# Half of the first keys loaded through GpSimd's casting queue instead of SyncE's queue, with new instruction orders

## The chip, the cores and the metric

The kernel runs on one core of a Trainium2 chip. A core has five engines with instruction rows of their own: PE (TensorE, matrix multiplies; PEld is its weight load), DVE (VectorE), ACT (ScalarE), POOL (GpSimd) and SP (SyncE). DMAs are issued from SP, ACT or POOL and share 16 DMA engines. Those that POOL issues here also change the type of the data on the way (float32 to bfloat16). The metric is device time of one execution in microseconds (us); lower is better.

## What is computed

Pooled attention over 8 batches and 8 heads (576 positions, head size 64; keys and values are averaged over 8 neighbouring positions, so 72 of each), and then a gated feed-forward net: a hidden layer of 1024 with ReLU, a convolution over three positions, a sigmoid gate, and an output layer of 512.

```
def _attn_ref(q, k, v):
    k_p = k.reshape(B, H, Sp, pool, D).mean(axis=3)
    v_p = v.reshape(B, H, Sp, pool, D).mean(axis=3)
    scores = scale * np.matmul(q, k_p.transpose(0, 1, 3, 2))
    scores = scores - np.max(scores, axis=-1, keepdims=True)
    attn = np.exp(scores)
    attn = attn / (np.sum(attn, axis=-1, keepdims=True) + 1e-09)
    return np.matmul(attn, v_p)

def _moe_ref(x, w_in, conv_w, w_out):
    h = np.maximum(x @ w_in, 0.0)
    hp = np.concatenate([zeros, h, zeros], axis=1)
    for k in range(K):
        conv_out += conv_w[k][None, None, :] * hp[:, k:k + S, :]
    gate = 1.0 / (1.0 + np.exp(-conv_out))
    return h * gate @ w_out
```

## The kernel before

The kernel is written as a graph of some 1040 small operations. Each is a Python closure that issues a handful of instructions, with a list of the operations it needs. `Graph.order` walks the table `ORDER`: an entry is twice an operation's number plus 0 or 1, the bit choosing between two engines where an operation may run on either; -1 puts in a spare, a dummy matmul (`fill`, L424) that computes nothing of the result. `FORMS` picks for some PE operations between a form with few wide matmuls and one with many narrow ones, and `PLACES` gives the buffer or PSUM bank. The tables fix the row of every engine; each engine takes its row strictly in order, and an instruction waits until what it needs is done.

The batches go in four groups of two. For each batch: the values are pooled in three additions and spread over masked columns (`prep_v`, L511 and L515, DVE). The keys are pooled; for the first two batches by matmuls against a pool matrix (`prep_k`, L431 and L441) with a copy out of PSUM (`copy_k`, L456), for the other batches by additions (L464) and turning matmuls with copies (L483, L504). The queries are transposed on PE (`prep_q`, L541 in the wide form, L545 in the narrow) and copied (`copy_q`, L559), or for two batches transposed by DMA (L553). Then for each tile of up to 128 positions: scores (`att_scores`, L620 wide, L607 narrow), maximum (L633, DVE), subtraction (L653 on PE or L645 on DVE), exponential (L682, ACT), transposition (L692 with the copy L706, or the DMA L701), product with the values (L717), reciprocal (L730), division (L745 on DVE, or eight parts at L738 on ACT), and transposition of the result (L762 with the copy L770, or the DMA L754). The feed-forward part of a batch: the hidden layer (`ffn_in`, L775, PE), ReLU (L784, ACT), and the convolution. This runs on PE (L939) with tanh (L964) for most of the first batches, or, for blocks of four 128-row pieces listed in `TAPS` (batches 4 to 7), as two multiply-adds on DVE, the taps (`ffn_tap`, L911), with the gate function on ACT (L921). Taps read columns beyond the tile's ends, which two small copies (`ffn_wrap`, L859 and L860, on POOL or ACT) fill. The gate is multiplied in (`ffn_times`, L989, DVE), and the output layer (L997, PE) is copied out of PSUM (L1008) and stored (L1020).

All loads but three are casting DMAs of POOL, in POOL's row: L284 for keys and queries of one batch, L291 for keys of a pair, L317 and L320 for values, L327 and L335 for weights. The exceptions concern batch 0. Its keys come in two pieces of two partition-major quarters each (`heads` 0 to 2 and 2 to 4), and its queries in two pieces along the row (`cs` 0 to 4 and 4 to 9). Both key pieces and the first query piece are loaded as float32 by SP (`load_raw`, L299) into room of `hT`, and cast to bfloat16 by DVE or ACT (`cast_raw`, L306) in steps of two quarters. The second query piece goes by POOL's casting queue. In `add_load` one condition (L1073) makes this choice. `prep_k` of batch 0 runs in two halves of 18 matmuls, the first needing the first key piece, the second the other; L1199 names the operation of each piece.

PE's row before begins with 15 fills, then 8 matmuls of the first query piece, the 36 of both key halves, the remaining 8 of the first query piece with the 20 of the second, and then the scores of the first tile.

Of the kernel before, what the change touches and what calls it, by code (L numbers as in the profile page):

```python
# [33 lines left out]
class Graph:  # L34
# [148 lines left out]
def kernel(  # L183
# [883 lines left out]
    def add_load(kind, b, key, share=1.0, after=(), **part):  # L1067
# [5 lines left out]
        if b == 0 and (kind == "k" or part["cs"].start == 0):  # L1073
            heads, cs = part.get("heads", slice(0, 4)), part.get("cs", slice(0, C))
# [424 lines left out]
```

## Time and profile before

| what | us |
|---|---|
| median of three runs | 213.53 |
| lowest, highest | 212.31, 215.35 |
| the profiled execution, its own time | 213.68 |
| span of that execution, first to last instruction | 211.7 |
| busy in it: PE / DVE / ACT / POOL | 198.9 / 190.5 / 167.2 / 36.7 |

The time of an execution holds the span and what lies around it. Busy times come from the one profiled execution. A matmul's duration is that of its way through the array, and the next one starts before it ends, so a busy PE may still have room. In a group's row stand the source line, the engine, the operation, the tiles, the count, the busy us, the mean duration in ns of one, and after the bar the idle time of the engine ahead of these instructions, with what ended it.

### The profile page before, as it was taken

How to read it: one execution, taken by the hardware profiler on the slowest of the kernel's cores; microseconds unless marked ns; L12 is line 12 of the kernel's file. 1: busy time of each engine (PE TensorE's matmuls, PEld its weight loads, DVE VectorE, ACT ScalarE, POOL GpSimd, SP SyncE). 2: the span in 40 equal slices, each digit the busy share in tenths (PEclk: the TensorE clock that was granted, in tenths of full speed). 3: DMA queues.
4: the chain of work that ended last, by engine and by line, in shares of the span. 5: the costliest groups of instructions: out<-in, count | busy, mean ns of one | idle time of the engine just before them, and what ended most of it. 6: DMA issues, size and time to landing. Idle time of an engine off the chain costs nothing.

```text
span 211.7 us, 6644 instructions
## 1 busy us (share of the span) xinstructions
PE 198.9 (94%) x2726; PEld 136.4 (64%) x2746; DVE 190.5 (90%) x338; ACT 167.2 (79%) x345; POOL 36.7 (17%) x60
## 2 busy tenths in 40 slices
PE   4899999999999999999999899999999999999990
PEld 1468788765688876776778675666666656654450
DVE  7879988999999999999998989999999999999520
ACT  2558677998999869999979977989899997889030
POOL 8604630052131110200000021000014400202000
PEclk9999999999999999999999999999999999999997
DMA  6999999999999999879663646756646626204985
GB/s 212 222 205 206 208 206 208 208 207 205 208 206 208 202 179 202 177 139 156 130 92 69 147 96 78 173 104 151 122 96 133 113 64 149 53 0 103 261 259 171
DMA packets 48834, 33.47 MB, mean 158 GB/s; under 512 B 28300, under 2 KB 43812, under 8 KB 48804
## 3 DMA queue, kind: packets, MB, share of 16 engines
q0 software_dynamic: 15216, 15.40, 44.6%
q1 hardware_dynamic: 32432, 15.93, 35.9%
q10 hardware_dynamic: 1156, 1.72, 2.8%
q8 instruction: 21, 0.34, 0.6%
q14 instruction: 9, 0.07, 0.1%
HBM read 32.52 MB, written 9.44 MB: 198 GB/s over the span
## 4 chain that ended last, share of the span: by engine, by line
PE 68%; DVE 19%; issue 5%; ACT 4%; DMA 2%; DVEq 0%; ACTq 0%
PE psum L997 25%; PE psum L775 22%; PE psum L717 5%; PE psum L939 3%; DVE negm L633 3%; DVE v L511 2%; PE psum L692 2%; DMA eT<-e 2%; PE psum L424 2%; DVE sd L645 2%; DVE gT L981 2%; PE psum L620 2%; DVE gT L989 1%; PE psum L653 1%; PE psum L762 1%
## 5 line engine op out<-in xcount | busy, mean ns | idle before, releaser
L775 PE MATMUL psum<-xT,w_in_sb 128*128 128x288 bf16 x512 | 72.0, 286 | 0.2
L997 PE MATMUL psum<-w_out_sb,gT 128*128 128x512 bf16 (+1 forms) x276 | 65.6, 373 | 1.4 <-issue 0.6
L775 PEld LDWEIGHTS <-w_in_sb 128*128 128x128 bf16 x512 | 47.8, 98 | 15.3
L784 ACT ACTIVATE hT<-psum 128x576 bf16<-128x576 f32 x64 | 41.1, 669 | 8.0 <-PE psum L775 7.8
L997 PEld LDWEIGHTS <-gT 128*128 128x128 bf16 x296 | 27.5, 98 | 26.5 <-DVE gT L989 0.5
L633 DVE TENSOR_REDUCE negm<-psum 128x8 f32<-128x576 f32 (+2 forms) x37 | 27.4, 750 | 2.0 <-ACT e L682 0.9
L921 ACT ACTIVATE gT<-tg,ratio 128x576 bf16<-128x576 f32 x28 | 21.6, 795 | 2.2 <-DVE tg L911 2.1
L911 DVE SCALAR_TENSOR_TENSOR tg<-hT,ratio,tg 128x576 f32<-128x576 bf16 x28 | 22.3, 813 | 0.7
L911 DVE SCALAR_TENSOR_TENSOR tg<-hT,ratio 128x576 f32<-128x576 bf16 x28 | 22.2, 812 | 0.2 <-ACT gT L921 0.2
L859 POOL COPY hT<-hT 128x126 bf16<-128x126 bf16 x7 | 5.7, 808 | 93.8 <-ACT hT L784 74.9
L989 DVE TENSOR_TENSOR gT<-gT,hT 128x2304 bf16<-128x2304 bf16 x16 | 21.6, 1354 | 0.2
L645 DVE TENSOR_TENSOR sd<-psum,negm 128x576 f32<-128x576 f32 x27 | 19.9, 751 | 0.6
L717 PE MATMUL psum<-vm,eT 128*128 128x65 bf16 (+5 forms) x240 | 19.0, 222 | 0.9 <-DMA eT<-e 0.9
L738 ACT ACTIVATE x<-psum,r 128x64 bf16<-128x64 f32 (+1 forms) x80 | 17.6, 352 | 2.8 <-DVE r L730 2.7
L682 ACT ACTIVATE e<-sd 128x576 bf16<-128x576 f32 x27 | 18.6, 703 | 0.4 <-DVE sd L645 0.2
L745 DVE TENSOR_TENSOR x<-psum,r 128x512 bf16<-128x512 f32 (+1 forms) x27 | 18.2, 682 | 0.5
L717 PEld LDWEIGHTS <-eT 128*128 128x128 bf16 (+1 forms) x240 | 15.1, 100 | 5.3 <-DMA eT<-e 1.7
L939 PE MATMUL psum<-hT,dw 64*64 64x288 bf16 (+2 forms) x576 | 17.0, 256 | 0.3 <-ACT qT L559 0.2
L939 PEld LDWEIGHTS <-dw 64*64 64x64 bf16 x576 | 13.9, 107 | 3.4 <-issue 2.3
L424 PE MATMUL psum<-gT 128*128 128x448 bf16 x40 | 13.1, 433 | 3.2 <-DVE gT L1106 2.8
L1008 ACT COPY osb<-psum 128x512 f32<-128x512 f32 x24 | 14.3, 600 | 1.2 <-PE psum L997 1.2
L511 DVE TENSOR_TENSOR v<-v 128x1280 bf16<-128x1280 bf16 (+2 forms) x24 | 12.9, 538 | 0.2
(95 smaller groups left out, 244.8 us busy)
## 6 DMA issues: line engine op xcount, KB each, us to landing
out_dram<-osb SPq DMA_DIRECT2D x54, 128.0 KB, 2.5
v<-in_v_dram POOLq DMA_DIRECT2D x8, 512.0 KB, 12.6
qp<-in_q_dram POOLq DMA_DIRECT2D x7, 576.0 KB, 15.3
kk<-in_k_dram POOLq DMA_DIRECT2D x3, 1152.0 KB, 13.7
out_dram<-qp ACTq DMA_DIRECT2D x12, 128.0 KB, 3.4
hT<-in_k_dram SPq DMA_DIRECT2D x2, 576.0 KB, 5.2
w_in_sb<-in_moe_w_in_dram POOLq DMA_DIRECT2D x2, 512.0 KB, 13.7
w_out_sb<-in_moe_w_out_dram POOLq DMA_DIRECT2D x1, 1024.0 KB, 23.7
```

The lines of the kernel that those rows point to most:

```text
L633: nc.vector.tensor_reduce(out=a["m"][0:rows], in_=a["s"][0:rows, :, 0:2 * KW].rearrange("p a (h s) -> p a h s", s=Sp), axis=AX.X, op=OP.ma ...
L645: nc.vector.tensor_tensor(out=a["d"][0:rows], in0=a["s"][0:rows, :, 0:2 * KW].rearrange("p a (h s) -> p a h s", s=Sp), in1=a["m"][0:rows]. ...
L682: nc.scalar.activation(out=dst, in_=src, func=ACT.Exp,)
L717: nc.tensor.matmul(out=a["o"][lo:hi, h // 4, (h % 4) * (D + 1):(h % 4 + x1 - x0) * (D + 1)], lhsT=a["eT"][:, j, lo:hi], rhs=buf("vm", b)[: ...
L745: nc.vector.tensor_tensor(out=a["x"][0:rows].rearrange("p (a h d) -> p a h d", a=2, d=D), in0=ov[:, :, :, 0:D], in1=r[0:rows].unsqueeze(3) ...
L775: nc.tensor.matmul(out=banks(ps)[:, j, 0:SC], lhsT=w_in_block(dc, fb), rhs=buf("xT", g)[:, dc, i * S + j * SC:i * S + (j + 1) * SC], start ...
L784: nc.scalar.activation(out=h_of(b)[:, fb].rearrange("p (a s) -> p a s", a=2), in_=banks(ps)[:, :, 0:SC], func=ACT.Relu, scale=1.0 if (b, f ...
L911: nc.vector.scalar_tensor_tensor(out=acc, in0=h, scalar=w, in1=acc if tap else mid, op0=OP.mult, op1=OP.add)
L921: nc.scalar.activation(out=gate, in_=acc_of(b, fb, ps), func=squash(b, fb), scale=ratio[:, 1, fb:fb + 1])
L939: nc.tensor.matmul(out=banks(pss[r ^ c])[c * D:(c + 1) * D, j, lo:hi], lhsT=dw[r * D:(r + 1) * D, tap * n_fb + fb, :], rhs=hT[r * D:(r + 1 ...
L989: nc.vector.tensor_tensor(out=gate, in0=gate, in1=h_of(b)[:, four], op=OP.mult)
L997: nc.tensor.matmul(out=bank(ps)[0:rows, columns], lhsT=buf("gT", g)[:, fb, t * P:t * P + rows], rhs=w_out_sb[:, fb, columns], start=(fb == 0),
```

## The change

`add_load` now lets only the first key piece of batch 0 (`heads` from 0) go by SP and a cast; the second (`heads` 2 to 4) falls through to the general case, a casting DMA of POOL (`load_k`, L284) straight into the bfloat16 tile. So the graph has one operation less: the SP load with its cast operation is replaced by one load. The tables `ORDER`, `FORMS` and `PLACES` are new from the first entry to the last; all the planner's other settings are as they were.

```
-        if b == 0 and (kind == "k" or part["cs"].start == 0):
+        if b == 0 and (part["heads"].start == 0 if kind == "k" else part["cs"].start == 0):
             heads, cs = part.get("heads", slice(0, 4)), part.get("cs", slice(0, C))
             d = add({"SP": 0.5}, key, lambda: load_raw(raw, heads, cs), land=(0.6, kb * share, RATE_FIRST))
             cast = []
...
     ORDER = (
-        0, 12, 10, 24, 16, 4, 44, 28, 8, 36, 14, 32, 46, 19, -1, -1, -1, -1, 21, 7,
+        0, 14, 4, 22, 42, 10, 12, 8, -1, -1, -1, -1, -1, -1, -1, 6, 40, 30, 34, 36,
...
     FORMS = (
-        0, 0, 0, 0, 1, 1, 1, 1, 0, 0, 0, 0, 0, 1, 1, 0, 1, 1, 0, 0, 1, 0, 1, 0, 0, 0, 0, 1, 0, 0, 0, 1, 1, 1, 1, 1, 1, 1, 0, 1,
+        1, 0, 0, 0, 1, 1, 1, 0, 0, 0, 0, 1, 1, 1, 1, 0, 0, 0, 1, 1, 0, 0, 0, 1, 1, 0, 0, 1, 0, 0, 0, 1, 1, 1, 1, 1, 1, 1, 0, 1,
...
```

Counted over the whole rows: fourteen wrap pairs (L859 and L860) stand 7 on ACT and 7 on POOL before, 2 and 12 after. DVE has 4 of the wide query copies (L559) before and 2 after, 7 and 5 of the wide output copies (L770), 26 and 25 of the wide divisions (L745); ACT has 6 and 8, 10 and 12, and 72 and 80 parts of divisions (L738). Of the casts of batch 0, DVE has one of the keys before and one of the queries after; ACT has one of the keys and two of the queries before, and one of each after. The number of fills is 40 in both.

PE's row after begins with 8 fills, the 18 matmuls of the first key half, 4 fills, the 16 of the first query piece, the 18 of the second key half, the 20 of the second query piece, and then the scores of the first tile in the narrow form.

The places of which the prediction speaks, with the names of the program's tiles: POOL's row behind the constants at the program's start (`ident` the identity, `mask` the head mask, `gT` whose spare room holds the pool matrix, `qp` the queries, `kk` the keys). Before:

```order
masks.py:197 MEMSET ident 128x128
masks.py:199 ISA
masks.py:199 AFFINE_SELECT ident<-ident 128x128
L362 MEMSET mask 128x15
L364 AFFINE_SELECT mask<-mask 128x15 x2
L343 AFFINE_SELECT gT_122<-gT_122 64x9x72 x2
L284 DMA qp_76<-in_q_dram 128x4x320
```

and after:

```order
L284 DMA kk_78<-in_k_dram 128x2x576
masks.py:197 MEMSET ident 128x128
masks.py:199 ISA
masks.py:199 AFFINE_SELECT ident<-ident 128x128
L362 MEMSET mask 128x15
L364 AFFINE_SELECT mask<-mask 128x15 x2
L343 AFFINE_SELECT gT_122<-gT_122 64x9x72 x2
L284 DMA qp_76<-in_q_dram 128x4x320
```

The key load stands ahead of everything else; the other seven rows keep their order. DVE's row at the end of its set-up, where the first results of PE come in (`ident_k` the scaled identity, `pick` its rearranged columns, `kT` the pooled keys, `qT` the transposed queries). Before:

```order
L359 COPY gT_122<-gT_122 64x9x72
L384 TENSOR_SCALAR ident_k<-ident 128x128
L387 COPY pick<-ident_k 128x2x16 x4
L306 CAST kk_78<-hT_116 128x1152
L456 CAST kT_82<-psum 64x2x72
L559 COPY qT_79<-psum 128x2x256
L559 COPY qT_79<-psum 128x2x320
L633 TENSOR_REDUCE negm_95<-psum 128x8
```

and after:

```order
L306 CAST qp_76<-hT_117 128x2x256
L339 MEMSET kT_82 128x288
L376 TENSOR_SCALAR vm_90<-mask 128x15
L376 TENSOR_SCALAR vm_91<-mask 128x15
L376 TENSOR_SCALAR vm_92<-mask 128x15
L376 TENSOR_SCALAR vm_93<-mask 128x15
L376 TENSOR_SCALAR vm_94<-mask 128x15
L456 CAST kT_86<-psum 64x2x72 x3
L559 COPY qT_80<-psum 128x2x320
L633 TENSOR_REDUCE negm_97<-psum 128x8
```

The key cast is gone from DVE and a query cast is there; `ident_k` and `pick` stand some 40 rows later, behind the first attention tiles. ACT's row from its first cast on. Before:

```order
L306 CAST qp_76<-hT_117 128x2x256 x2
L306 CAST kk_78<-hT_116 128x1152
L559 COPY qT_79<-psum 128x2x256
L456 CAST kT_82<-psum 64x2x72 x3
L559 COPY qT_79<-psum 128x2x320
```

and after:

```order
L306 CAST kk_78<-hT_116 128x1152
L456 CAST kT_86<-psum 64x2x72
L306 CAST qp_76<-hT_117 128x2x256
L559 COPY qT_80<-psum 128x2x256 x2
L559 COPY qT_80<-psum 128x2x320
```

The one key cast left on ACT is that of the first piece, ahead of the query cast.

More of the change, by code (lines that the diff above doesn't have):

```diff
@@ L72 @@
     ORDER = (
[54 rows of a table removed]
[54 rows of a table added]
     )
     FORMS = (
-        0, 0, 0, 0, 1, 1, 1, 1, 0, 0, 0, 0, 0, 1, 1, 0, 1, 1, 0, 0, 1, 0, 1, 0, 0, 0, 0, 1, 0, 0, 0, 1, 1, 1, 1, 1, 1, 1, 0, 1,
+        1, 0, 0, 0, 1, 1, 1, 0, 0, 0, 0, 1, 1, 1, 1, 0, 0, 0, 1, 1, 0, 0, 0, 1, 1, 0, 0, 1, 0, 0, 0, 1, 1, 1, 1, 1, 1, 1, 0, 1,
     )
     PLACES = (
[18 rows of a table removed]
[18 rows of a table added]
     )
@@ L1072, in add_load @@
             toks[b] = token("qp", b)
-        if b == 0 and (kind == "k" or part["cs"].start == 0):
+        if b == 0 and (part["heads"].start == 0 if kind == "k" else part["cs"].start == 0):
             heads, cs = part.get("heads", slice(0, 4)), part.get("cs", slice(0, C))
```

144 rows, old and new, of tables (ORDER, PLACES) are left out of this document.

## The prediction

> **What bounds the kernel now.** First the busy time by stage (columns: stretch in us, its length, busy us and instruction count of PE, PEld, DVE, ACT and POOL, granted clock, DMA share, GB/s), cut where the chain changes its nature: end of the loads' casts, first score matmul, first hidden-layer matmul, first tap, last gate, last matmul.
>
> ```profile
> 9.44:11.71 2.27, 2.10 (x65) 2.03 (x66) 0.85 (x3) 1.67 (x6) 0.00 (x0) 1.00 1.19 185
> 11.71:28.09 16.38, 16.35 (x346) 12.22 (x346) 14.90 (x31) 11.29 (x19) 6.67 (x9) 1.00 1.23 207
> 28.09:125.00 96.91, 94.40 (x1631) 71.12 (x1633) 92.61 (x168) 85.02 (x175) 11.50 (x20) 1.00 1.01 172
> 125.00:197.04 72.04, 71.31 (x626) 44.06 (x632) 70.87 (x101) 63.49 (x141) 10.62 (x14) 1.00 0.53 105
> 197.04:205.90 8.86, 8.78 (x48) 4.62 (x48) 2.96 (x5) 2.24 (x4) 0.00 (x0) 1.00 0.89 271
> 205.90:211.70 5.80, 0.00 (x0) 0.00 (x0) 0.42 (x1) 0.00 (x0) 0.00 (x0) 0.81 0.58 174
> ```
>
> From 11.71 us on PE is busy nearly throughout, and DVE almost as much: 70.87 of 72.04 us in the late stretch, where PE has 71.31. Two engines are full together, so relief of one alone is worth little, and a wait on either shows. The clock is 1.00 until the matmuls end; it plays no part.
>
> Second, the chain that ended last, at its start and inside the middle stretch (start us, us, what).
>
> ```profile
> 7.47 0.59 DVE ident_k L384
> 8.09 0.70 DVE pick L387 x4
> 8.79 0.61 DVE kk L306
> 9.44 1.33 PE psum L431 x36
> 10.80 0.27 ACT kT L456
> ...
> 11.71 0.41 PE psum L620 x4
> 12.12 0.65 PE psum L424 x3
> ...
> 90.18 0.81 DVE v L511
> 91.00 0.77 DVE negm L633
> ```
>
> Up to 9.4 us the chain is DVE's list of small set-up work, ending in the cast of the first keys; then PE pools the keys (L431), ACT copies them (L456), and the first scores (L620) start at 11.71. Around 90 us the chain runs on DVE; late it is PE.
>
> Third, the first loads and casts themselves, from the timeline, and the landing times (the last number of an issue group, and the min/median/max of SyncE's three loads).
>
> ```profile
> 1.83 0.52 SPq L299 DMA_DIRECT2D hT<-in_k_dram  x1
> 3.59 0.89 POOL L284 DMA_DIRECT2D qp<-in_q_dram  x1
> 5.27 1.15 DVE L381 COPY mask_wide<-mask 128x960 bf16<-128x960 bf16 x1
> 5.74 0.81 POOL L284 DMA_DIRECT2D kk<-in_k_dram  x1
> 6.05 1.14 ACT L306 CAST qp<-hT 128x512 bf16<-128x512 f32 x2 [3.66 <-DMA hT<-in_q_dram]
> 8.40 0.98 DVE L306 CAST kk<-hT 128x1152 bf16<-128x1152 f32 x1
> 8.62 1.15 ACT L306 CAST kk<-hT 128x1152 bf16<-128x1152 f32 x1 [1.43 <-DMA hT<-in_k_dram]
> 10.59 0.95 PE L541 MATMUL psum<-ident,qp 128*64 128x128 bf16 x28
> ...
> qp<-in_q_dram POOLq DMA_DIRECT2D x1, 320.0 KB, 6.6
> kk<-in_k_dram POOLq DMA_DIRECT2D x1, 576.0 KB, 10.6
> DMA to landing us min/median/max: 3.7/4.7/6.8
> ```
>
> SyncE's second key half, issued at 1.83, landed 6.8 us later, at 8.6, where ACT stops waiting for it and casts until 9.77. The casting load of the other five ninths of the first queries, issued at 3.59, landed 6.6 us later, at 10.2. The first key half (3.7 us) was there by about 4.5, and was cast only at 8.40: DVE was not free.
>
> **The change part by part.** (1) *The load moves.* GpSimd issues it first of all, at the 0.8 us where its first memset of the identity stood, and pushes everything behind it back by one issue, about 0.8 us (0.89 and 0.81 above): identity, mask, pool matrix, and the casting loads of queries, first values and second keys on the same queue. SyncE's queue then holds one key half and the queries, in the same order. The landing is the unknown. From below: bytes shared with SyncE's two loads, 3.7 to 4.7 us as those took, so 4.5 to 5.5. From above: 10.6 us as the second keys' casting load took with three loads ahead of it, so 11.4. I take 6.6 us, the query load of the same queue, which likewise shared the engines with SyncE's loads: 7.4, inside the 8.6 of before.
>
> The first queries' second part comes behind it on the queue. Before, that part landed at 10.2 after the same four pieces of data (two key halves, two query parts); after, the same four. I take 10.2 again; bounds 9.4 (the 0.8 us of later issue gained back as the values no longer push in) and 11.1 (10.2 and one issue).
>
> A rule speaks against the move. The Trainium skill, "SBUF — State Buffer", section "SBUF: two separate sides", holds that a GpSimd-issued DMA waits for its descriptors while VectorE runs a copy in a two-port mode, and the next section gives 620 ns alone against 3100 ns beside such a copy. Here the issue at 5.74 stood beside the 1.15 us copy at L381 and took 0.81, against 0.89 for one beside memsets: the trace doesn't show the rule. By the rule's figures the landing would be an estimated 2.5 us later, 9.9 in place of 7.4.
>
> (2) *The casts go.* ACT's 1.15 us cast of the second half (8.62 to 9.77) is gone, and DVE's 0.98 us cast of the first moves to ACT, which has been idle for 3.66 us by 6.05. DVE takes one of the two query casts (1.14 for two), and its identity scaling and `pick` (0.59 and 0.70, on the chain) go to a place behind the first attention tiles. DVE's set-up list is no longer in front of the keys. In PE's row stand now: first key half, 4 fills, first query part, second key half, second query part, first scores. The fills and key half are done by about 7 (cast from 4.5 to 5.65, 18 of the 36 pool matmuls, 0.66 us); the second key half by 8.1 (7.4 and 0.66); so the second query part, landing at 10.2, is late next. Its 20 of 28 matmuls take 0.68, and the scores start at 10.9 in place of 11.71: **0.8 us gained**. With the bounds, 9.4 gives 1.6 gained; 11.1 gives 0.1 lost. If the keys land at 11.4, 0.66 of pooling, three copies on DVE in place of ACT's three at 0.27, and 0.68 put scores at 13.5: 1.8 lost.
>
> (3) *The new orders shift work between engines.* Counted in the rows of both orders, priced by the groups of before (name, shapes, count, busy us, mean ns; two lines give min/median/max ns instead):
>
> ```profile
> L559 DVE COPY qT<-psum 128x1152 bf16<-128x1152 bf16 x4 | 3.0, 740 | 0.0
> L770 DVE COPY xT<-psum 128x512 bf16<-128x512 bf16 x7 | 2.9, 420 | 0.4 <-PE psum L762 0.2
> L745 DVE TENSOR_TENSOR x<-psum,r 128x512 bf16<-128x512 f32 x26 | 17.6, 682 | 0.5
> L738 ACT ACTIVATE x<-psum,r 128x64 bf16<-128x64 f32 x72 | 15.9, 357 | 2.4 <-DVE r L730 2.3
> L559 ACT COPY qT<-psum 128x1152 bf16<-128x1152 bf16 x6 | 6.7, 1120 | 0.3 <-PE psum L541 0.2
> L770 ACT COPY xT<-psum 128x512 bf16<-128x512 bf16 x10 | 5.8, 583 | 2.4 <-PE psum L762 2.4
> L483 ACT CAST kT<-psum 64x288 bf16<-64x288 f32 x8 | 3.0, 392 | 0.1
> L859 ACT COPY hT<-hT 128x126 bf16<-128x126 bf16 x7 | 2.2, 310 | 0.1
> L859 POOL COPY hT<-hT x7: 292/827/1472, 125.8 to 190.0; 128x126 bf16<-128x126 bf16 x7
> L911 DVE SCALAR_TENSOR_TENSOR tg<-hT,ratio x28: 765/810/900, 124.2 to 192.2; 128x576 f32<-128x576 bf16 x28
> ```
>
> DVE gives up the key cast (0.98), two query copies (2 x 0.74), two output copies (2 x 0.42), one division (0.68) and a narrow query copy (0.3, 512/1152 of 0.74): 4.3. It takes one query cast (0.5, between 512/1152 of its 0.98 and half of ACT's 1.14) and five key copies (two small at ACT's 0.27, three at 0.39): 2.2. Net **-2.1 us on DVE**. ACT gives up a query cast, those five copies and ten wrap copies (0.57 + 1.7 + 10 x 0.31 = 5.4) and takes two query copies, two output copies, a division in eight parts and the narrow copy (2 x 1.12 + 2 x 0.58 + 8 x 0.36 + 0.5 = 6.8): +1.4. GpSimd takes the ten wrap copies at about 0.82: +8.2, on an engine with 10.62 busy of the late 72.04 us.
>
> What is DVE's relief worth? Late, where PE is as full, nothing. In the middle, where the chain runs on DVE, up to all of it. Bounds 0 and 2.1; I take half, **1.0 gained**, since PE has 94.40 of 96.91 there. ACT's 1.4 has cover: 85.02 of 96.91 and 63.49 of 72.04 us busy.
>
> (4) *Fills.* PE's row holds dummy matmuls (L424) where a gap was planned: 40 in both, but 28 instead of 25 after the first scores, and 12 instead of 8 after the first hidden layer matmul. At 0.22 each (0.65 for three) three more cost 0.7 if PE had work, nothing if it waits; I take **0.6 lost**, as PE waits little. PE's other work: half of one query preparation in 18 wide instead of 36 narrow matmuls, and scores of three tiles the other way; at 0.41 a tile that can't be over 1.2 either way, taken as nothing.
>
> (5) *What counting can't give.* Each of the new orders' thousand steps waits for others; the measure is PE's idle time of before after 28 us, 2.51 + 0.73 = 3.2 us. A new order could close all of it, or have twice as much; I take a little more, **0.6 lost**, bounds -3.2 and +3.2.
>
> The end is alike: after the last two gates (L989) PE's row has the same 32 wide and 16 half output matmuls, so the 8.86 and 5.80 us of the last two stretches stay.
>
> Sum: -0.8 - 1.0 + 0.6 + 0.6 = -0.6. The profiled execution took 213.68 us, of which
>
> ```profile
> span 211.7 us, 6644 instructions
> ```
>
> leaves 2.0 around it, unchanged; it stands 0.15 above the median, 213.53. So 213.68 - 0.6 = 213.1.
>
> **The rivals.** *Slower, by the wraps.* Ten wrap copies go to GpSimd, where a pair takes 1.65 (2 x 0.827) instead of 0.62 on ACT. DVE's taps (L911) of that block can't begin before. If in all five pairs the first tap stands next in DVE's row, DVE waits 1.03 each, 5.2 in all, in the stretch where it has 1.2 idle: 213.1 + 5.2 = 218.3, over 2% slower. It decides only if all five wait; four give 217.2. For it: GpSimd's copies stretch to 1.47. Against: none of before's seven pairs there shows a DVE wait, and taps of several blocks interleave. That GpSimd and VectorE hinder each other here is also what the Trainium skill, "SBUF — State Buffer", section "Who interferes with whom", holds for a VectorE instruction with two SBUF inputs beside a GpSimd read, and L859's 292 to 1472 agrees; L911, 765 to 900, bounds the loss on DVE's side at 0.1 for each tap it meets. Chance 0.06. *Slower by other waits of the new orders*: as much idle again as before had, 3.2, with the start's 1.8 lost and no relief for DVE: 213.68 + 3.2 + 1.8 + 0.6 = 219.3. Chance 0.12.
>
> *The late load.* The keys land at 11.4, the start loses 1.8 in place of gaining 0.8: 213.1 + 2.6 = 215.7, within 2%. For it: the second keys took that on this queue; against: they had three loads ahead of them, these have none. Chance 0.12. By the rule of (1) it would be 9.9 and, with the pooling, copies and the second query part behind it, scores at about 12: 214.2.
>
> *Nothing at the start.* The second query part holds the scores and the gain is used up by a fill or a copy: 213.9. Chance 0.15.
>
> *Faster.* All of DVE's 2.1 counts, the start gains 1.6 and the idle falls by half, 1.6, fills costing nothing: 213.68 - 5.3 = 208.4. Chance 0.12.
>
> **How the numbers follow.** The forecast, 0.43, with the late load and the unchanged start makes 0.70 for within 2%, which is about what a measurement of this kernel can tell from no change (212.31 to 215.35 over three runs, 1.4%), here 209.3 to 217.8. Slower 0.06 + 0.12 = 0.18, faster 0.12. The range leaves out about a tenth at each side: from 209.4, most of the faster case beyond it, to 217.9, just short of the two slow ones.
>
> **What would show it.** Right: the first L620 or L607 near 10.9 us, behind the second query part and not behind the keys; GpSimd's first load landing by 8; DVE's busy time about 2 us below before's, GpSimd's about 8 above; PE's idle from 28 us to the last gate near 4. Wrong: L431 waiting for the key load at 9 us or later; a DVE wait at L911 for L859 or L860; PE idle over 6 us between 28 and 197.

## The result and the profile after

| what | before | after |
|---|---|---|
| median, us (4 runs each) | 213.49 | 215.67 |
| lowest, highest | 212.31, 215.35 | 215.22, 217.20 |
| profiled execution, its span | 213.68, 211.7 | 215.22, 213.5 |
| busy PE / DVE / ACT / POOL | 198.9 / 190.5 / 167.2 / 36.7 | 200.6 / 189.0 / 168.4 / 40.3 |

The change is slower by 1.4%: ratio 1.0136, 95% interval 1.0104 to 1.0168. A second measurement, beside later experiments, gave 1.0118 (1.0060 to 1.0177). In the tables below medians are over all runs, while ratios leave disturbed ones out, so the two can differ.

The busy time of after in the stretches in which before was shown (same columns):

```profile
9.44:11.71 2.27, 1.16 (x46) 0.90 (x40) 0.69 (x3) 1.20 (x3) 0.86 (x2) 1.00 1.17 167
11.71:28.09 16.38, 15.56 (x352) 11.36 (x344) 14.69 (x31) 12.02 (x25) 6.18 (x8) 1.00 1.23 207
28.09:125.00 96.91, 95.18 (x1656) 71.81 (x1646) 92.16 (x173) 84.42 (x165) 12.30 (x22) 1.00 1.02 169
125.00:197.04 72.04, 71.75 (x631) 44.08 (x630) 69.84 (x99) 63.33 (x142) 12.94 (x22) 1.00 0.58 113
197.04:205.90 8.86, 8.65 (x42) 3.83 (x41) 4.24 (x6) 3.04 (x6) 0.00 (x0) 1.00 0.71 203
205.90:211.70 5.80, 1.69 (x16) 1.27 (x13) 0.85 (x2) 0.59 (x1) 0.00 (x0) 0.82 0.80 230
```

PE has work at 206 us where before it had none. It is idle for longer up to 28 us (1.16 busy of 2.27, 15.56 of 16.38), and for less afterwards. Two places of the timeline show where it stands still. The first is the start:

```profile
1.32 0.84 POOL L284 DMA_DIRECT2D kk<-in_k_dram  x1 [0.80 <-POOLq L1483]
4.97 0.77 POOL L284 DMA_DIRECT2D qp<-in_q_dram  x1
...
10.84 0.75 PE L541 MATMUL psum<-ident,qp 128*64 128x128 bf16 x20 [1.11 <-DMA qp<-in_q_dram]
11.52 0.33 PE L607 MATMUL psum<-kT,qT 64*64 64x72 bf16 x16
```

The issue groups of the same start (the last number is us to landing):

```profile
qp<-in_q_dram POOLq DMA_DIRECT2D x1, 320.0 KB, 5.8
kk<-in_k_dram POOLq DMA_DIRECT2D x1, 288.0 KB, 6.1
```

The keys land at 1.3 + 6.1 = 7.4. The second query part is issued at 4.97, where before it was at 3.59; it lands at 10.8, and PE waits for it. The second place is near 90 us (bracket: idle before, and what ended it):

```profile
84.68 1.32 SPq L701 DMA_TRANSPOSE eT<-e  x1
86.05 2.50 SPq L1020 DMA_DIRECT2D out_dram<-osb  x4
88.65 3.82 SPq L553 DMA_TRANSPOSE qT<-qp  x1
...
90.42 0.44 PE L692 MATMUL psum<-ident,e 128*128 128x128 bf16 x5
91.78 1.04 PE L997 MATMUL psum<-w_out_sb,gT 128*128 128x512 bf16 x4 [0.92 <-issue]
```

"issue" means that PE waited for nothing that the profile knows of. `eT` are the transposed exponentials, `osb` the output buffers.

To see how far a kernel has come, the matmul columns that PE has still to start are counted from the trace's weight loads and divided by a round 2400 a us (in after's trace one 512-column matmul of L997 mostly starts 0.216 us behind the other, which is 2370). The difference to before, in us of PE work that a kernel is behind, is good to some 0.4, since the orders differ:

```
from, us              30    60    80    90    95   100   110   150   200
after                1.0   0.4   0.4   1.1   1.8   1.3   2.0   1.0   1.7
after, again         1.6   1.0   1.3   1.8   1.9   1.6   2.3   1.3   2.1
load alone          -0.2  -0.1   0.0  -0.1   1.0   1.8   2.3   1.3   1.3
load, L553 late     -0.2  -0.1   0.0  -0.1  -0.2   0.3   0.8  -0.4  -0.2
orders alone         0.6  -0.1   0.0   0.7   1.4   1.2   1.6   0.6   1.3
orders, short keys   0.4  -0.1   0.0   0.2   0.2  -0.2   0.1  -0.9  -0.2
```

The start and the stretch from 85 to 100 us carry the loss.

### The profile page after: what moved, and what is told of

It is laid out like the page before. It is cut to its first block, busy times and chain, and to the rows that moved or that the text cites. A ratio compares the mean times of both kernels' runs of the same rounds, so it can differ in the third digit from the quotient of the medians.

```text
span 213.5 us, 6693 instructions
## 1 busy us (share of the span) xinstructions
PE 200.6 (94%) x2756; PEld 136.6 (64%) x2756; DVE 189.0 (89%) x337; ACT 168.4 (79%) x342; POOL 40.3 (19%) x71
## 5 line engine op out<-in xcount | busy, mean ns | idle before, releaser
L775 PE MATMUL psum<-xT,w_in_sb 128*128 128x288 bf16 x512 | 70.2, 286 | 0.4 <-DVE x L745 0.2
L997 PE MATMUL psum<-w_out_sb,gT 128*128 128x512 bf16 (+1 forms) x296 | 67.0, 373 | 1.1 <-issue 0.9
L775 PEld LDWEIGHTS <-w_in_sb 128*128 128x128 bf16 x512 | 48.3, 98 | 15.3 <-issue 1.2
L997 PEld LDWEIGHTS <-gT 128*128 128x128 bf16 x296 | 27.8, 98 | 29.2 <-issue 1.1
L859 POOL COPY hT<-hT 128x126 bf16<-128x126 bf16 x12 | 6.4, 534 | 98.1 <-ACT hT L784 92.6
L738 ACT ACTIVATE x<-psum,r 128x64 bf16<-128x64 f32 (+1 forms) x88 | 19.2, 328 | 1.8 <-DVE r L730 1.6
L745 DVE TENSOR_TENSOR x<-psum,r 128x512 bf16<-128x512 f32 (+1 forms) x26 | 17.9, 687 | 0.6
L1008 ACT COPY osb<-psum 128x512 f32<-128x512 f32 x24 | 14.1, 599 | 1.1 <-PE psum L997 1.0
L964 ACT ACTIVATE tg<-psum 128x576 bf16<-128x576 f32 x18 | 11.7, 652 | 2.8 <-PE psum L939 2.8
## 6 DMA issues: line engine op xcount, KB each, us to landing
v<-in_v_dram POOLq DMA_DIRECT2D x8, 512.0 KB, 11.1
qp<-in_q_dram POOLq DMA_DIRECT2D x7, 576.0 KB, 14.1
```

What stands on the lines that cost most here:

```text
L738: nc.scalar.activation(out=a["x"][0:rows, n * D:(n + 1) * D], in_=ov[:, n // 4, n % 4, 0:D], func=ACT.Identity, scale=r[0:rows, n // 4, n ...
L775: nc.tensor.matmul(out=banks(ps)[:, j, 0:SC], lhsT=w_in_block(dc, fb), rhs=buf("xT", g)[:, dc, i * S + j * SC:i * S + (j + 1) * SC], start ...
L997: nc.tensor.matmul(out=bank(ps)[0:rows, columns], lhsT=buf("gT", g)[:, fb, t * P:t * P + rows], rhs=w_out_sb[:, fb, columns], start=(fb == 0),
```

## The experiments

All compare with the kernel before on the same chip.

| kernel | median, us | ratio | 95% interval |
|---|---|---|---|
| load alone | 215.91 | 1.0098 | 1.0065 to 1.0131 |
| orders alone | 214.48 | 1.0060 | 1.0041 to 1.0080 |
| new start, old rest | 218.68 | 1.0227 | 1.0164 to 1.0290 |
| old start, new rest | 213.94 | 1.0044 | 1.0029 to 1.0059 |
| before, 288 KB more on GpSimd's queue | 216.04 | 1.0133 | 1.0091 to 1.0174 |
| load alone, L553 late | 213.67 | 1.0019 | 0.9991 to 1.0047 |
| before, L553 late | 213.56 | 1.0013 | 1.0000 to 1.0027 |
| after, 64 rows more | 219.72 | 1.0304 | 1.0251 to 1.0357 |
| after, stores early | 216.19 | 1.0156 | 1.0115 to 1.0196 |
| orders alone, stores early | 214.49 | 1.0057 | 1.0035 to 1.0079 |
| after, 12 fills out | 216.80 | 1.0117 | 1.0077 to 1.0158 |
| orders alone, 12 fills out | 214.38 | 1.0059 | 1.0030 to 1.0088 |
| orders alone, 288 KB more | 215.34 | 1.0109 | 1.0072 to 1.0146 |
| orders alone, short keys | 213.06 | 0.9991 | 0.9969 to 1.0013 |
| after, short keys | 215.86 | 1.0144 | 1.0123 to 1.0165 |

**Load or orders.** *Load alone*, in the rows of SyncE, GpSimd and ACT, everything else as before (k0 and q0 are the first parts of batch 0's keys and queries, k0+ and q0+ the second):

```
-  SP: k0, q0, k0+      POOL: ident, mask, pool matrix, q0+, ...
+  SP: k0, q0           POOL: k0+, ident, mask, pool matrix, q0+, ...
-  ACT: cast of k0+
```

> The old orders, slots and forms; only the load of the second half of the first keys goes from SyncE's queue to GpSimd's, first on that queue, and its cast on ScalarE is gone. Theory A (the new orders cost the time, the load by itself is nearly free): the keys land near 7.4 us as in the changed kernel, the second query part about 0.8 later than before because GpSimd's row is 0.84 longer ahead of it, first scores between 11.2 and 12.2 us, total within 0.6 of the kernel before (213.0 to 214.1). Theory B (the moved load costs the time, by delaying the second query part or by slowing VectorE's set-up): first scores at 12.7 or later and a total of 214.9 to 215.7, like the changed kernel.

*Orders alone* is after with this undone:

```
+  SP: k0, q0, k0+      POOL: ident, mask, pool matrix, q0+, ...
+  ACT: cast of k0+ behind the cast of the first query part
```

> The new orders, slots and forms; only the load goes back to SyncE's queue, third on it, with its cast on ScalarE behind the cast of the first query part. Theory A (the new orders cost the time): 215.0 to 216.2, as the changed kernel, with the gap of PE near 91 us in the trace. Theory B (the load costs it): 213.0 to 214.0.

Neither theory had it: both parts cost, and nearly add up (1.0098 x 1.0060 = 1.0158). In the load alone the first scores start at 11.58, no later than before's 11.71, and it is not behind until 90 us; its whole loss comes between 90 and 110.

**Start or rest.** The two orders were joined at the first hidden-layer matmul (L775), with buffers found anew where the halves meet:

```
-  ORDER = after's
+  ORDER = after's up to the first L775, then before's (and the reverse, with the old load)
```

> The new load and the new orders up to the first hidden layer matmul of batch 0 (L775), the old orders from there (36 fills in all, 32 of them at the start where the new order has them). Theory A1 (the loss lies behind the first 30 us: transitions and the stall near 91 us): 213.2 to 214.2. Theory A2 (the start loses, 1.0 us of PE work behind at 30 us, and it is never made up): 214.4 to 215.2.

> The old load and the old orders up to the first hidden layer matmul, the new orders from there (44 fills in all). Theory A1 (the loss lies behind the first 30 us): 214.9 to 216.2, with the gap of PE near 91 us. Theory A2 (the start loses): 213.2 to 214.3.

Both theories missed the first (218.68; PE waits 2.57 us for ACT's L1008 at 97.68 in it, a wait that the load alone shows below), and the second came out where A2 had it. That doesn't show A2's reason, since ahead of the gap near 91 us its PE program is 24 rows shorter, and the gap is gone. The pair also moves the load along with the start, so it does not tell the parts apart.

**Why a load at 1.3 us costs at 90.** The two pages' rows of GB/s (40 slices of the span, 5.3 us each), before and load alone:

```profile
GB/s 212 222 205 206 208 206 208 208 207 205 208 206 208 202 179 202 177 139 156 130 92 69 147 96 78 173 104 151 122 96 133 113 64 149 53 0 103 261 259 171
```

```profile
GB/s 212 155 198 207 207 206 208 207 207 206 208 207 207 204 110 141 165 251 122 159 103 61 153 109 82 141 109 162 113 103 147 102 74 148 52 0 97 255 260 178
```

From the third slice to the fourteenth it stays near 207: GpSimd's queue is full to some 74 us. Before, the second slice held 222, as SyncE's loads came on top; with the load moved it holds 155, and each of GpSimd's later loads lands later, by 1.0 to 1.5 us from 38 to 73 us. The query load of batch 6 (576 KB), issued at 58.69 in before, landed after 14.1 us, at 72.8; issued at 58.48 in the load alone it took 15.4, to 73.8. What waits for it is SyncE's DMA transposition of batch 6 (L553), which starts 0.1 us behind the landing in both. SyncE's row before:

```profile
72.83 3.64 SPq L553 DMA_TRANSPOSE qT<-qp  x1
81.29 1.20 SPq L701 DMA_TRANSPOSE eT<-e  x1
82.54 2.51 SPq L1020 DMA_DIRECT2D out_dram<-osb  x4
```

and in the load alone, with two rows of its PE and ACT below:

```profile
73.92 10.72 SPq L553 DMA_TRANSPOSE qT<-qp  x1
84.75 2.67 SPq L701 DMA_TRANSPOSE eT<-e  x1
87.47 2.98 SPq L1020 DMA_DIRECT2D out_dram<-osb  x4
...
95.50 0.58 ACT L1008 COPY osb<-psum 128x512 f32<-128x512 f32 x1 [1.72 <-DMA out_dram<-osb]
96.14 1.02 PE L997 MATMUL psum<-w_out_sb,gT 128*128 128x512 bf16 x3 [1.46 <-ACT osb L1008]
```

GpSimd issues the next key pair (1152 KB) at 73.51 in before, 0.7 behind L553; in the load alone at 73.31, 0.6 ahead of it. Issued behind that load, the transposition holds SyncE for 10.72 us in place of 3.64. The stores behind it come 5 us late, ACT waits for an output buffer, and PE for ACT.

Three runs test this. One more load on the queue, behind all that the start waits for:

```
     def load_w_in(j):
+        if j == 0:
+            load_more()     # 288 KB of keys, cast into a part of hT that nothing reads
```

> The kernel before, with its keys still loaded by SyncE, and one more load of the same 288 KB on GpSimd's queue (the same rows, cast into a part of hT that nothing reads) just ahead of the first half of w_in, so behind all that the start waits for. Theory Q (GpSimd's queue is full without a break from 5 to 73 us, so that 288 KB more on it make every later load land about 1.0 to 1.4 us later; the query load of batch 6 then lands behind the issue of the next key pair, the DMA transposes of L553 run beside that load for some 10 us in place of 3.6, and SyncE's transposes and stores behind them come late): L553's issue takes over 8 us, first scores as before at 11.7, total 214.0 to 216.5, and runs that lie further apart than before's. Theory S (the moved load costs at the start): 212.5 to 213.6, L553's issue below 5 us.

L553, issued 1.5 us behind the key pair's load, held SyncE for 8.56 us; first scores came at 11.68 as before, and the time was 216.04: the loss without the moved load. Then the transposition out of the way, with its control:

```
-  SP: L553, L701 (eT), 4 x L1020, ...
+  SP: L701 (eT), 4 x L1020, L553, ...
```

> The load moved in the old orders, as in the run of the load alone (1.0098 of before), and in addition the first DMA transposes of L553 (batch 6) behind the next eT transposes and the four output stores on SyncE's queue. Theory Q (they block SyncE for 10.7 us beside the key pair's load): the eT transposes are issued near 81.3 again and not at 84.7, PE loses under 1.0 between 85 and 100 us, total 212.6 to 214.0. Rival (the lost time is the load's elsewhere, at the start or in PE's own row): as with the load alone, 214.5 to 216.

> The kernel before with only that move of L553 behind the eT transposes and the four stores: the control for it. Both theories: 212.3 to 214.0, since before's L553 runs in 3.6 us where nothing else is on the queues; if the later place costs something by itself (it then meets the loads of v at 86 us), up to 214.5.

With L553 late the load costs 1.0019 against the control's 1.0013. PE's busy time from 90 to 100 us, in the load alone and with L553 late:

```profile
90.00:95.00 5.00, 3.79 (x109) 2.98 (x109) 4.55 (x8) 2.88 (x5) 0.00 (x0) 1.00 0.99 224
95.00:100.00 5.00, 3.81 (x33) 2.33 (x37) 3.74 (x8) 4.36 (x13) 0.00 (x0) 1.00 0.67 155
```

```profile
90.00:95.00 5.00, 5.00 (x122) 3.63 (x121) 4.84 (x10) 4.66 (x9) 0.00 (x0) 1.00 1.25 172
95.00:100.00 5.00, 4.54 (x62) 2.62 (x58) 4.90 (x12) 4.71 (x14) 0.00 (x0) 1.00 1.13 174
```

Theory Q holds for the old orders: 7.60 busy of 10 becomes 9.54. In the new orders L553 stands at 88.65, where it took 3.82, so this cost can't be theirs.

**The gap near 90 us.** The trace lists 21 packets of 16 KB of instructions, and PE's program has some 5500 rows, one packet to about 251 of them (eight packets between rows 3260 and 5268 in after). The gap stands at the same row in kernels in which different instructions stand there. Numbers from the traces; the row 252 ahead marks the packet's turn. The gap is counted from the start of the weight load ahead of it to the start of the next, so it is longer than the idle time in the profile's bracket:

```
kernel                  PE at row   packet  behind   GpSimd's loads    PE's gap ahead of
                          2752      starts             landed          row 3004 to 3006
before                    85.72     86.88    1.16    85.5               none
load, L553 late           85.50     87.12    1.62    83.8               none
load alone                85.52     88.87    3.35    87.9               0.64 (16 L607, ahead of the 6th)
after                     86.12     89.14    3.02    88.8 and 89.2      1.19 (L997)
after, again              86.74     89.67    2.92    89.3 and 89.8      0.99 (L997)
orders alone              85.69     88.69    3.00    88.4 and 88.8      1.18 (L997)
after, stores early       86.85     89.97    3.12    89.6 and 90.1      1.21 (L997)
orders, stores early      85.09     88.19    3.09    87.8 and 88.3      1.18 (L997)
orders, 288 KB more       86.48     89.28    2.81    88.9 and 89.4      0.93 (L997)
orders, short keys        85.24     86.26    1.02    84.7 and 85.0      none
after, short keys         87.06     87.98    0.92    87.1 and 87.4      none
old start, new rest       85.84     88.84    3.00    88.5 and 89.0      none (PE there at 91.6)
after, fills out          86.25     89.26    3.02    88.9 and 89.4      none (PE there at 92.0)
orders, fills out         86.80     89.45    2.65    89.1 and 89.6      none (PE there at 92.3)
```

Where there is a gap, PE goes on 1.4 to 1.5 us after the packet has landed. In the last three kernels the packet is late too. But their program is 24 rows shorter up to there, so four wide matmuls (L997) stand in front of row 3004, and PE comes to it only 1.5 to 1.7 us after the packet has landed. The Trainium skill, "Runtime: NRT & Kernel Launch", section "Instruction fetch mechanics", has blocks of 16 KiB, which an engine's sequencer fetches through its own DMA queue while it runs the one before, "mostly hidden". The trace agrees on size and way (21 packets of 16 KB on a queue of their own); here it was not hidden, by up to 1.2 us.

A first test moved the fetch, by 32 tiny matmuls (64 rows) in the first fills:

```
     def fill(ps):
         nc.tensor.matmul(out=bank(ps)[:, 0:448], ...)
+        for _ in range(3 if len(filled) <= 8 else 2 if len(filled) <= 12 else 0):
+            nc.tensor.matmul(out=bank(ps)[0:32, 0:16], lhsT=blank[:, 0:32], rhs=blank[:, 0:16], ...)
```

> The changed kernel with 32 tiny dummy matmuls more (32x16, 64 rows of PE's program) among the first 12 fills, where PE waits for the second query part anyway (1.11 us idle at 10.84). Theory F (the gap ahead of row 3004 of PE's program is the fetch of PE's next 16 KB of instructions, which starts at 89.14 because the queues are full from 85 us): the fetch is asked for 64 rows earlier, about 1.5 us, where only GpSimd's loads run; no gap over 0.6 us near L997 at 90.6, and a gap if any at row 3004 of the new count, 64 rows earlier in the program; total 0.6 to 1.2 below the changed kernel, 214.2 to 215.0. Rival W (that L997 waits for something that belongs to it, a gate or a bank): the gap of 1.1 stays at the same instruction, total 215.2 to 216.5.

L997 followed its predecessor without a gap, as theory F has it, though the packet was still 2.5 us behind its turn. But the eight first fills took from 2.79 to 8.12 us, first scores slipped to 15.04, and the time (219.72) says nothing on the gap. Then the four stores that stand ahead of the fetch:

```
-  SP: 2 x L1020, L701 (eT), 4 x L1020, L553, ...
+  SP: 6 x L1020 (from 52 to 57 us), L701 (eT), L553, ...
```

> The changed kernel once more, beside the three below on the same chip: 215.0 to 216.5, with the gap of about 1.1 us ahead of L997 near 90.6 us.

> The changed kernel with the four output stores that stand behind the eT transposes of 84.68 us on SyncE's queue put right behind their copies (52 to 57 us), where SyncE has nothing else to do. Theory F (row 3004 of PE's program begins a block of instructions, and its fetch starts only at 89.14, 58 rows ahead of need, because transposes, stores and loads fill the queues from 84.7 us): the fetch starts before 88, no gap over 0.6 at row 3004, 0.8 to 1.3 less than the changed kernel unless the stores delay the loads of 55 to 62 us by more than their slack. Rival W (L997 waits for a gate or a bank, or the loss comes from elsewhere): the gap stays, time within 0.4 of the changed kernel.

> The same move of the four stores in the kernel with the new orders and the old load (orders alone: 1.006 of before). Theory F: the 0.006 is for the most part the gap of 1.18 at 90.16, so 212.4 to 213.7, within 0.3% of before. Rival W: as the orders alone, 214.0 to 215.0.

The changed kernel came out as expected (215.23, gap 0.99). Theory F was wrong on the stores: the gap stayed in both kernels, and neither became faster. The stores are not what delays the packet. What is common to the late ones is GpSimd's loads beside SyncE's transpositions up to 88 us and beyond, so the loads were cut:

```
-        nc.gpsimd.dma_start(out=buf("kk", g)[:, :, 0:POOL * D], in_=rows...)
+        n = 4 if g == 3 else C
+        nc.gpsimd.dma_start(out=buf("kk", g)[:, 0:n, 0:POOL * D], in_=rows...[:, 0:n])
```

> The new orders with the old load; the last pair's key load (batches 6 and 7) brings only 4 of its 9 parts, 512 of 1152 KB, so the output of these two batches is of stale keys. GpSimd's queue runs empty some 3 us earlier, near 85.5 to 86 us in place of 88.8. Theory F2 (the fetch that PE needs at row 3004 of its program starts only when GpSimd's loads have drained: 2.7 to 3.3 us behind row 2752 in the seven kernels whose loads last beyond 87.5 us, 0.9 to 1.6 in the five whose queue was empty by then): the fetch starts within 1.7 us of row 2752, no gap over 0.6 at row 3004, 213.0 to 214.0. Rival (something else delays it): the gap of 1.1 to 1.2 stays, 214.2 to 215.0.

> The changed kernel with the same shorter last key load. Theory F2: no gap over 0.6 at row 3004, 0.6 to 1.2 below the changed kernel's 215.2 to 215.7, so 214.0 to 215.0; what is then left over before is the start, about 1. Rival: 215.0 to 216.5 with the gap.

The orders with short keys, PE at the place of the gap (lines one higher than in after):

```profile
89.53 0.44 PE L693 MATMUL psum<-ident,e 128*128 128x128 bf16 x5
90.03 0.81 PE L998 MATMUL psum<-w_out_sb,gT 128*128 128x512 bf16 x3
```

The packet comes 1.0 us behind row 2752, no gap, and 0.9991 in place of 1.0060: with fewer bytes in that load the orders' cost is gone. The kernel before was not run with short keys, so part of this may be a gain that any of the kernels would have. How much is the gap itself and how much the rest of the crowded queues isn't separated; the three kernels whose gap went while the packet stayed late kept most of their cost (1.0044 and 1.0059 against 1.0060, 1.0117 against 1.0118). With the load moved as well, short keys also end the gap, yet the time stays at 1.0144, above the 214.0 to 215.0 that theory F2 had. In that trace what is left is at the start.

**The start.** Same orders, GpSimd's queue with and without the keys in front: in the six traced kernels with the new start and the moved load (the 64 rows aside) the second query part lands at 10.8 to 11.8, PE stands still 1.1 to 2.6 us for it and first scores start at 11.5 to 12.6; in the five with the new start and the old load it lands at 9.7 to 10.6 and scores start at 10.8 to 11.3. After in its second profiled execution, and the orders alone:

```profile
11.46 0.75 PE L541 MATMUL psum<-ident,qp 128*64 128x128 bf16 x20 [2.29 <-DMA qp<-in_q_dram]
12.14 0.32 PE L607 MATMUL psum<-kT,qT 64*64 64x72 bf16 x16
```

```profile
10.61 0.75 PE L541 MATMUL psum<-ident,qp 128*64 128x128 bf16 x20 [0.17 <-DMA qp<-in_q_dram]
11.29 0.33 PE L607 MATMUL psum<-kT,qT 64*64 64x72 bf16 x16
```

The standstill can cost twice. In after with short keys (the last number but two is the granted clock):

```profile
8.00:12.00 4.00, 1.44 (x56) 1.17 (x50) 0.77 (x4) 1.43 (x3) 2.31 (x4) 1.00 1.21 175
12.00:16.00 4.00, 4.00 (x34) 2.32 (x23) 2.86 (x6) 1.38 (x3) 0.00 (x0) 0.57 1.22 208
```

Behind 2.56 idle us the granted clock was 0.57; PE was 2.2 us behind before at 30 us, where after was 1.0 and 1.6.

Does the late queue cost anything in the new orders too? Orders alone with the 288 KB more of above, start untouched:

> The new orders with the old load and 288 KB more on GpSimd's queue behind the loads that the start waits for, just ahead of the first half of w_in. Theory Q2 (in the new orders too the moved load costs by making GpSimd's full queue late behind 24 us): 215.3 to 217.0, like the changed kernel or more. Theory S2 (in the new orders the load costs at the start, by the 0.4 to 0.7 that the first v load comes later, and the late queue has slack, since no DMA transposes stand at 73 us): 214.0 to 215.0, as the orders alone.

215.34, the low edge of Q2, and its interval touches that of the orders alone. One wait of its trace is the queue's:

```profile
32.00 1.15 PE L782 MATMUL psum<-xT,w_in_sb 128*128 128x288 bf16 x8 [0.51 <-DMA w_in_sb<-in_moe_w_in_dram]
```

So both ways are open to the load in the new orders; their shares are not settled.

**The fills.** The 12 dummy matmuls behind the first hidden-layer matmul taken out of ORDER, from after and from the orders alone:

```
-  ..., 984, -1, ...
+  ..., 984, ...       (12 entries of -1)
```

> The changed kernel without the 12 dummy matmuls (L424) behind the first hidden layer matmul, where before has 8. The prediction's theory of the fills (each costs 0.22 where PE has work, four more of them 0.9): at least 0.9 and up to 2.6 less than the changed kernel, 213.0 to 214.8. Rival (they stand in gaps of PE): within 0.4 of the changed kernel. The rows of PE's program are 24 fewer from there, which by theory F moves the place where PE needs its next block by 24 rows and may by itself shift the gap near 90 us by some tenths.

> The new orders with the old load (1.006 of before, gap of 1.18 at 90.16), without the 12 dummy matmuls behind the first hidden layer matmul, which puts PE's program 24 rows back from there. Theory F (the gap is a block of instructions that comes late; 24 rows less and it is gone, as in the trace of the changed kernel without these fills): no gap over 0.6 near 90 us, 0.5 to 1.1 less than the orders alone, 213.2 to 214.0. Rival (the gap is covered later, the orders' cost is elsewhere): 214.2 to 215.0.

No gain in either (1.0117 against 1.0118; 1.0059 against 1.0060), though the gap ahead of row 3004 was gone in both; for the orders that is what the rival said. In the trace of the orders without fills PE's clock fell, which may hide a small gain:

```profile
44.00:48.00 4.00, 2.55 (x83) 1.97 (x82) 3.81 (x8) 3.98 (x15) 1.15 (x1) 0.95 1.24 206
48.00:52.00 4.00, 3.87 (x20) 2.04 (x21) 2.84 (x6) 2.28 (x4) 0.00 (x0) 0.62 1.24 206
```

With the fills PE was busy 3.99 of the first four us and the clock stayed 1.00. In after without fills PE was busy only 2.89 of the same four us, and the clock stayed 1.00 too. So the fills stand in gaps; that they hold the clock isn't shown, as it fell in one of two traces without them.

## Why the forecast was wrong

The time lay within the range, but the sign was wrong: 0.6 us faster was forecast, 2.2 us slower came. The sum had two gains, 0.8 at the start and 1.0 from DVE's relief. Neither came, and the cost of 288 KB more on a full queue was not in the sum. By steps:

1. *The load moves.* The landing, 7.4, came out exactly. What failed is the sentence on the second query part, "I take 10.2 again". It came at 10.8, and at 11.1 to 11.8 in the other kernels with this start: it was issued 1.38 us later, not one issue of 0.8, since the load began at 1.32, half a microsecond behind the place at 0.8 that was counted on, and took 0.84; and 288 KB stood in front of it on its queue. That put first scores at 11.52 or 12.14, not 10.9. With the old load the new orders do start scores at 10.8 to 11.3, so the load took the early start away. But an early start is not yet time gained, as the sum took it: at 30 us the orders alone are 0.6 us of PE work behind before, not ahead.
2. *What the sum left out.* The move was priced by its issue and by two landings, not by the queue: 288 KB from a queue with room onto one that is full to 74 us. This is the step that has no term. The runs price it at 1.0% in the old orders (load alone), 1.3% by itself there (before with 288 KB more), and 0.5% by itself in the new orders (1.0109 against 1.0060, intervals that touch). In the new orders the moved load as a whole costs 0.6 to 0.8% (1.0118 and 1.0136 against 1.0060). The row that would have told was on the page before: GB/s near 207 in twelve slices on end.
3. *DVE's relief*, 1.0 forecast, was worth nothing that shows. DVE had 1.5 us less, but all of it at the start, where it waits: 0.00 to 12.00 us has 7.48 busy in after and 9.07 in before. GpSimd had 3.6 more, not the 8 expected.
4. *Fills*, 0.6 lost: wrong in kind. They filled waits; without them nothing was won.
5. *Other waits of the new orders*, 0.6 lost, bounds 3.2: no run has this term alone. The orders alone, with all the terms of the orders in them, cost 1.3 us (1.0060), where the three terms -1.0, 0.6 and 0.6 make 0.2. The measure chosen, PE's idle time from 28 us on, doesn't show the cost: it fell from 3.2 to 2.0 (1.73 and 0.29 in the stretches above), 0.92 of which is the gap that no row of any order shows.

The rival of the wraps is out: GpSimd took them, L859's mean was 534 ns, and DVE waits for one of them in after, for 0.2 us. The late load's rival had the time nearly right (215.7) by luck: keys at 11.4, where they came at 7.4. The rival "nothing at the start" had the mechanism of the start right, the second query part holding the scores, but not the time (213.9). The Trainium skill's rule ("SBUF — State Buffer", section "SBUF: two separate sides") that GpSimd's descriptors wait while VectorE copies in a two-port mode was not put to the test by the moved load: its issue, at 1.32 to 2.16, ran beside two VectorE memsets and no copy. The second query part's issue, at 4.97, ran beside copies and took 0.77, so the trace still doesn't show the rule.

What isn't settled: why the packet of instructions starts late beside those loads and transpositions (that it does is shown, the order among the queues isn't), and how the load's 0.6 to 0.8% in the new orders divides between start and queue. No version tried beats the kernel before. The load alone with L553 late is level with it (1.0019, 0.9991 to 1.0047); with the new orders only short keys are, which leave out part of two batches' keys.

## What to carry to other kernels

Before moving a transfer to another queue, read how long that queue stays full: its bytes delay everything behind them, and the price can fall due where a late landing changes sides with another transfer, in the old orders here 70 us later. A load put first on a queue makes the second one late: count what waits for that. And a gap that no dependence explains may be the engine's own instructions: compare the program's row number, not the instruction, over several kernels.

## What the runs showed of the hardware

- PE's instructions came in packets of 16 KB for about 251 rows, asked for about one packet ahead. Where GpSimd's loads were all landed only 2.4 us or more behind the packet's turn, the packet started 2.7 to 3.4 us behind it, in place of 0.9 to 1.6, and in seven of ten such traces PE stood still for 0.6 to 1.2 us.
- A DMA transposition held SyncE for 3.6 us when it was issued 0.7 us ahead of a casting load of 1152 KB, and for 10.7 and 8.6 us when it was issued 0.6 and 1.5 us behind it.
- The granted clock was 0.57 and 0.62 in the four us behind four us with 2.6 and 1.5 us of idle PE; behind 2.3 idle us at the start of after's second execution it stayed 1.00.
